# A hand-written order for five engines, listed anew: linear attention and a folded feed-forward on one core

## The chip, the core and the metric

The kernel runs on one core of a Trainium2 chip. A core has five engines with a queue of their own each: TensorE (PE, with its weight loads as PEld), VectorE (DVE), ScalarE (ACT), GpSimd (POOL) and SyncE (SP, which here only issues DMAs). Each engine takes its instructions in the order in which the program lists them, and waits where one needs what another engine has not yet finished. The metric is the device time of one execution in microseconds, as the median of several runs.

## What is computed

```python
q_s = exp(q - max(q, axis=-1)); q_s /= sum(q_s, axis=-1) + 1e-9     # q: 8 x 8 x 576 x 64
k_s = exp(k - max(k, axis=2));  k_s /= sum(k_s, axis=2) + 1e-9
kv  = einsum('bhsd,bhse->bhde', k_s, v)
x   = einsum('bhsd,bhde->bhse', q_s, kv)      # then as 4608 tokens x 512
out = ((x @ w1) * (x @ w2)) @ w3 @ w_out      # w1, w2: 512 x 1024; w3: 1024 x 1024; w_out: 1024 x 512
```

Inputs and output are float32; the kernel works in float16 with float32 sums.

## The kernel before, in words

**The work.** w3 and w_out are folded into one matrix W3O (1024 x 512) first: for each of 8 row blocks ft, PE transposes w3 (step w3t.ft), an engine copies it out of PSUM (w3T.ft), PE multiplies it by w_out in two halves (pf.ft.0, pf.ft.1), and an engine scales it into W3O (W3O.ft).

The attention runs by batch b, 0 to 7. On the side of k: kmx (maximum over the sequence, as a tree of two-input steps for batches 0 to 3, as two reductions kmx.b.0 and kmx.b.1 after that), cba (a transpose and a reduction on DVE), cbx (four small copies on ACT that swap neighbouring groups of 32 partitions, line 509: "ScalarE's swap"), cb (DVE), ksub.b.0 and .1 (subtract), kexp.b.0 and .1 (exponential, ACT), vc.b.0 and .1 (v to float16, from batch 2), kv (PE), kve (ACT) and kv2 (DVE). On the side of q, in two parts p: qmx, qsub, qexp, qsm, qeps, qrc, qn; then q is turned, either on PE with a copy (qt and qT, batches 0 and 1) or by a transposing DMA that SP issues (qd.b.0 and qd.b.1, line 637, from batch 2). Then PE multiplies (xm.b.0, xm.b.1 and xt.b for the last 64 tokens of a batch), and xs and xts copy the result out of PSUM.

The feed-forward runs by chunk c, 0 to 7 for the 512 first tokens of each batch and 8 for the 8 x 64 tokens left. For a chunk there are 8 pairs of steps up.1 and up.0 (x @ w2, x @ w1; 8 matmuls of 256 columns in chunks 0 and 1, 4 of 512 in the others), bs (copies the up.1 product out of PSUM, line 323), ab (multiplies it by the up.0 product, DVE, line 794), and four times down (8 matmuls with W3O, line 801), os (copy out of PSUM) and st (store, two DMAs on SP).

**The order.** Nothing is ordered by the compiler: ORDER (line 77) lists all 794 steps by name, and Plan.run (line 48) emits them in that order, each on its engine. So the list sets the order within each engine's queue and nothing else; between engines only data and buffers order the work. PICKS (line 154) names the engine of those steps that can run on more than one. The buffers are rings: 4 PSUM banks "pab" for up (and for xt from batch 3), 2 "po" for down, pf and xm.b.1, 2 "att" for kv, qt and the other xm, 4 buffers each for bs and os. A step that takes a ring's buffer waits for the reader of its former content.

**The links.** Steps with two inputs in SBUF (kmx as a tree, ksub, qsub, qn, vc on POOL, qeps on DVE) are marked "port". Among the first LINKED steps of the list (line 75), when such a step stands on another engine than the marked step before it, its first instruction is made to wait for the last one of that step (lines 68 to 72, `link` in line 883).

**Loads.** HW lists two loads for SP, LOADS (line 216) those that POOL issues, LATE (line 223) those on SP after that. A load of POOL's list waits for the load eight places ahead of it; the first of LATE waits for the third from the end of LOADS (w1.3 in either order). A load into a buffer in use waits for its readers (line 393). In the names, w3.4 is 512 KB and w3.0 256 KB; loads of q, k and v are 1152 KB per batch.

**Fills.** `fill` (line 347) issues matmuls of zeros that nobody reads; FILL (line 149) puts so many of them ahead of the steps that it names, and "begin" ahead of all.

Of the kernel before, what the change touches and what calls it, by code (L numbers as in the profile page):

```python
# [82 lines left out]
pf.3.0 pf.3.1 kexp.0.1 w3t.1 kexp.0.0 k.2 kv.0 W3O.3 w3T.1 W3O.7 w3T.6 qmx.1.0 kve.0 kv2.0 pf.1.0
pf.6.0 xm.0.0 qsub.1.0 xs.0.0.0 xs.0.0.1 pf.6.1 pf.1.1 kmx.1.0 xm.0.1 qexp.1.0 xs.0.1.1 xs.0.1.0
up.1.0.0.0 bs.0.0.0 up.0.0.0.0 up.1.0.1.0 up.0.0.1.0 up.1.0.0.1 qsm.1.0 qeps.1.0 qrc.1.0 ab.0.0.0
cba.1 w1.3 v.1 q.1.1 qn.1.0 bs.0.1.0 up.0.0.0.1 qt.1.0 ab.0.1.0 up.1.0.1.1 up.0.0.1.1 cbx.1 cb.1
bs.0.0.1 ksub.1.0 ab.0.0.1 qT.1.0 q.2 bs.0.1.1 xt.0 up.1.0.0.2 ab.0.1.1 W3O.6 bs.0.0.2 up.0.0.0.2
ab.0.0.2 W3O.1 ksub.1.1 kexp.1.0 kmx.2.0 up.1.0.1.2 up.0.0.1.2 up.1.0.0.3 bs.0.1.2 up.0.0.0.3
up.1.0.1.3 bs.0.0.3 ab.0.0.3 down.0.0 xts.0.0 kexp.1.1 cba.2 ab.0.1.2 xts.0.1 cbx.2 cb.2 ksub.2.1
kv.1 kve.1 bs.0.1.3 kexp.2.1 os.0.0 down.0.1 ksub.2.0 v.2 up.0.0.1.3 kv2.1 qmx.1.1 xm.1.0 xs.1.0.0  # L90
xs.1.0.1 qsub.1.1 ab.0.1.3 down.0.2 up.1.1.0.0 up.0.1.0.0 up.1.1.0.1 qmx.2.1 qmx.2.0 os.0.1
up.0.1.0.1 bs.1.0.0 up.1.1.0.2 down.0.3 ab.1.0.0 kexp.2.0 qexp.1.1 qsm.1.1 qsub.2.1 k.3 v.3 q.3
qsub.2.0 vc.2.1 vc.2.0 qexp.2.1 qeps.1.1 bs.1.0.1 qexp.2.0 qsm.2.1 qrc.1.1 qsm.2.0 os.0.2 bs.1.0.2
qeps.2.0 up.0.1.0.2 kv.2 kve.2 ab.1.0.1 up.1.1.0.3 up.0.1.0.3 qn.1.1 qrc.2.0 kv2.2 qn.2.0 qeps.2.1
qt.1.16 qt.1.8 os.0.3 ab.1.0.2 bs.1.0.3 qrc.2.1 qn.2.1 st.0.0 k.4 qd.2.0 ab.1.0.3 qT.1.16 down.1.0
qmx.3.1 qT.1.8 qd.2.1 q.4 st.0.1 xm.1.1 down.1.1 xs.1.1.1 xs.1.1.0 xt.1 kmx.3.0 qmx.3.0 up.1.1.1.0
up.0.1.1.0 xts.1.1 xts.1.0 xm.2.0 bs.1.1.0 xs.2.0.0 xs.2.0.1 cba.3 ab.1.1.0 up.1.1.1.1 up.0.1.1.1
bs.1.1.1 ab.1.1.1 os.1.0 cbx.3 st.0.3 v.4 xm.2.1 xs.2.1.1 xs.2.1.0 cb.3 kmx.4.1 up.1.1.1.2
up.0.1.1.2 up.1.1.1.3 bs.1.1.2 vc.3.1 qsub.3.0 qsub.3.1 up.0.1.1.3 ksub.3.0 qexp.3.0 ab.1.1.2
qsm.3.0 bs.1.1.3 qexp.3.1 ab.1.1.3 up.1.2.0.0 up.0.2.0.0 up.1.2.0.1 bs.2.0.0 ksub.3.1 up.0.2.0.1  # L100
vc.3.0 q.5 st.0.2 ab.2.0.0 bs.2.0.1 kexp.3.0 up.1.2.0.2 up.0.2.0.2 up.1.2.0.3 qsm.3.1 ab.2.0.1
qmx.4.1 vc.4.1 up.0.2.0.3 bs.2.0.2 up.1.2.0.4 kexp.3.1 os.1.1 v.5 qeps.3.1 qeps.3.0 kmx.4.0 qsub.4.1
qexp.4.1 kv.3 qrc.3.1 qmx.4.0 ab.2.0.2 down.1.2 down.1.3 os.1.2 qrc.3.0 cba.4 qsm.4.1 bs.2.0.3 kve.3
os.1.3 up.0.2.0.4 up.1.2.0.5 ab.2.0.3 kv2.3 qn.3.1 xt.2 bs.2.0.4 up.0.2.0.5 up.1.2.0.6 qn.3.0
qsub.4.0 cbx.4 cb.4 ab.2.0.4 up.0.2.0.6 qd.3.1 st.1.1 qd.3.0 xts.2.1 qexp.4.0 bs.2.0.5 qmx.5.1
xts.2.0 bs.2.0.6 ab.2.0.5 xm.3.1 xm.3.0 xt.3 ab.2.0.6 xs.3.1.0 xs.3.0.1 xs.3.1.1 xs.3.0.0 xts.3.1
xts.3.0 up.1.2.0.7 up.0.2.0.7 up.1.3.0.0 up.0.3.0.0 bs.2.0.7 qeps.4.1 ksub.4.1 ksub.4.0 vc.4.0
kexp.4.1 qmx.5.0 ab.2.0.7 qrc.4.1 qsm.4.0 qeps.4.0 kexp.4.0 bs.3.0.0 up.1.3.0.1 k.5 kv.4 ab.3.0.0
kmx.5.1 qrc.4.0 q.6 st.1.2 qsub.5.1 st.1.3 st.1.0 up.0.3.0.1 up.1.3.0.2 up.0.3.0.2 down.2.0 down.2.1
k.6 qexp.5.1 bs.3.0.1 kmx.5.0 qmx.6.0 qmx.6.1 cba.5 bs.3.0.2 os.2.0 os.2.1 ab.3.0.2 cbx.5 kve.4 cb.5  # L110
qsub.5.0 ab.3.0.1 kv2.4 up.1.3.0.3 down.2.2 qsm.5.1 qn.4.0 qn.4.1 qd.4.0 qd.4.1 qexp.5.0 st.2.0 q.7
v.6 os.2.2 bs.3.0.3 down.2.3 os.2.3 up.0.3.0.3 qsub.6.0 xm.4.0 ab.3.0.3 xm.4.1 xt.4 xts.4.0 xs.4.1.0
xts.4.1 up.1.3.0.4 up.0.3.0.4 ksub.5.0 vc.5.1 xs.4.0.0 bs.3.0.4 kmx.6.0 ab.3.0.4 qeps.5.1 xs.4.0.1
kexp.5.0 kmx.6.1 xs.4.1.1 up.1.3.0.5 up.0.3.0.5 bs.3.0.5 up.1.3.0.6 up.0.3.0.6 bs.3.0.6 ab.3.0.5
up.1.3.0.7 up.0.3.0.7 qrc.5.1 qsm.5.0 ab.3.0.6 qeps.5.0 bs.3.0.7 qrc.5.0 ksub.5.1 qsub.6.1 kexp.5.1
vc.5.0 up.1.4.0.0 bs.4.0.0 up.0.4.0.0 up.1.4.0.1 st.2.1 qmx.7.1 cba.6 ab.3.0.7 down.3.0 qn.5.1
qsub.7.1 st.2.2 k.7 qmx.7.0 os.3.0 ab.4.0.0 qsub.7.0 qn.5.0 qexp.6.0 qexp.6.1 qsm.6.1 kv.5
up.0.4.0.1 up.1.4.0.2 bs.4.0.2 up.0.4.0.2 down.3.1 cbx.6 bs.4.0.1 ab.4.0.1 os.3.1 qexp.7.0 st.3.1
ab.4.0.2 cb.6 ksub.6.1 qsm.6.0 up.1.4.0.3 bs.4.0.3 up.0.4.0.3 ksub.6.0 qexp.7.1 ab.4.0.3 up.1.4.0.4
kmx.7.1 up.0.4.0.4 kve.5 kexp.6.1 qeps.6.0 bs.4.0.4 qeps.6.1 up.1.4.0.5 kv2.5 up.0.4.0.5 bs.4.0.5  # L120
ab.4.0.4 kexp.6.0 down.3.2 ab.4.0.5 qrc.6.1 qrc.6.0 qsm.7.0 qn.6.1 up.1.4.0.6 os.3.2 kmx.7.0
qeps.7.0 st.2.3 qd.5.0 vc.6.0 qd.5.1 st.3.2 v.7 up.0.4.0.6 bs.4.0.6 xm.5.1 qn.6.0 vc.6.1 xm.5.0
qd.6.1 st.3.0 up.1.4.0.7 xs.5.1.0 xs.5.1.1 ab.4.0.6 up.0.4.0.7 xs.5.0.1 bs.4.0.7 xs.5.0.0 qd.6.0
down.3.3 cba.7 ab.4.0.7 cbx.7 qrc.7.0 qsm.7.1 up.1.5.0.0 os.3.3 st.3.3 up.0.5.0.0 bs.5.0.0 qn.7.0
down.4.0 ab.5.0.0 qeps.7.1 cb.7 down.4.1 os.4.0 ksub.7.1 st.4.0 up.1.5.0.1 ksub.7.0 os.4.1 kexp.7.1
st.4.1 up.0.5.0.1 qrc.7.1 bs.5.0.1 qn.7.1 up.1.5.0.2 kexp.7.0 ab.5.0.1 down.4.2 bs.5.0.2 up.0.5.0.2
os.4.2 st.4.2 kv.6 ab.5.0.2 xt.5 up.1.5.0.3 kve.6 xts.5.0 qd.7.0 xts.5.1 kv2.6 up.0.5.0.3 bs.5.0.3
qd.7.1 vc.7.0 vc.7.1 up.1.5.0.4 ab.5.0.3 up.0.5.0.4 bs.5.0.4 up.1.5.0.5 ab.5.0.4 up.0.5.0.5 bs.5.0.5
up.1.5.0.6 ab.5.0.5 xm.6.0 xm.6.1 bs.5.0.6 xt.6 up.0.5.0.6 xs.6.1.1 xts.6.1 xs.6.1.0 xts.6.0
xs.6.0.0 up.1.5.0.7 xs.6.0.1 ab.5.0.6 up.0.5.0.7 bs.5.0.7 down.4.3 ab.5.0.7 up.1.6.0.0 os.4.3  # L130
down.5.0 st.4.3 bs.6.0.0 up.0.6.0.0 os.5.0 up.1.6.0.1 st.5.0 ab.6.0.0 down.5.1 bs.6.0.1 up.0.6.0.1
os.5.1 st.5.1 up.1.6.0.2 ab.6.0.1 up.0.6.0.2 bs.6.0.2 kv.7 ab.6.0.2 up.1.6.0.3 kve.7 kv2.7 down.5.2
bs.6.0.3 up.0.6.0.3 os.5.2 st.5.2 up.1.6.0.4 ab.6.0.3 up.0.6.0.4 bs.6.0.4 up.1.6.0.5 ab.6.0.4
up.0.6.0.5 bs.6.0.5 up.1.6.0.6 ab.6.0.5 up.0.6.0.6 bs.6.0.6 xm.7.0 xm.7.1 ab.6.0.6 xt.7 up.1.6.0.7
xs.7.1.1 xs.7.0.0 xs.7.1.0 xs.7.0.1 up.0.6.0.7 bs.6.0.7 xts.7.1 xts.7.0 down.5.3 ab.6.0.7 down.6.0
os.5.3 st.5.3 up.1.7.0.0 os.6.0 st.6.0 up.0.7.0.0 bs.7.0.0 up.1.7.0.1 ab.7.0.0 up.0.7.0.1 bs.7.0.1
down.6.1 ab.7.0.1 up.1.7.0.2 os.6.1 st.6.1 down.6.2 bs.7.0.2 up.0.7.0.2 os.6.2 up.1.7.0.3 st.6.2
ab.7.0.2 up.0.7.0.3 bs.7.0.3 up.1.7.0.4 ab.7.0.3 up.0.7.0.4 bs.7.0.4 up.1.7.0.5 ab.7.0.4 up.0.7.0.5
bs.7.0.5 up.1.7.0.6 ab.7.0.5 up.0.7.0.6 bs.7.0.6 up.1.7.0.7 ab.7.0.6 up.0.7.0.7 bs.7.0.7 up.1.8.0.0
# [80 lines left out]
]  # L220
# [699 lines left out]
```

## Time and profile before

| what | before |
|---|---|
| median of 3 runs | 243.56 us (243.51 to 243.75) |
| the profiled execution, its own time | 244.17 us |
| its span in the profile | 242.4 us |
| PE, DVE, ACT, POOL busy | 232.4, 179.7, 123.1, 106.3 us |
| first up step starts | 34.58 us |
| last matmul group starts | 231.25 us, for 7.09 us |
| DMA traffic | 45.67 MB, mean 188 GB/s |

The span runs from the first to the last instruction; what the execution's own time has above it lies around it. Busy times are sums of the instructions' durations. Matmuls overlap in the profile, so that a short gap of PE can hide in its busy time: the distance from one start to the next tells more. A row of the timeline has the start, the duration, the engine, the line, the operation, output and input tiles with shapes, and the number of instructions put together; in square brackets, when the engine was idle before it, for how long and what ended that. A row of a group has the busy time, the mean of one in ns, and the idle time before. "<-DMA qT<-en" means that the transfer which turns q ended the wait.

### The profile page before, as it was taken

To read this page: it belongs to the slowest core of one execution; us is meant where nothing else is said; L and a number is where in the kernel's file an instruction comes from. 1 tells how busy PE (TensorE), PEld (TensorE's weight loads), DVE (VectorE), ACT (ScalarE), POOL (GpSimd) and SP (SyncE) were. 2 spreads that over 40 slices of the span, in tenths; PEclk is the share of its full clock that TensorE was granted. 3 is DMA by queue.
4 is the path that set the end of the run, shared out by engine and by line. 5 is a ranking of instruction groups with operands and counts; after the bars stand their busy time and mean duration, and the time that the engine had idled before them with its cause. 6 is when DMAs were issued, how large, how long until landed. Compare 5 with 4: busy or idle time off the path is not lost.

```text
span 242.4 us, 4971 instructions
## 1 busy us (share of the span) xinstructions
PE 232.4 (96%) x1988; PEld 121.3 (50%) x1988; DVE 179.7 (74%) x270; ACT 123.1 (51%) x228; POOL 106.3 (44%) x72
## 2 busy tenths in 40 slices
...
GB/s 203 218 299 216 334 205 285 268 392 386 367 192 301 302 306 142 353 359 156 360 176 130 176 103 312 107 141 3 95 42 38 60 73 43 0 89 0 63 110 131
DMA packets 37895, 45.67 MB, mean 188 GB/s; under 512 B 15984, under 2 KB 22384, under 8 KB 37872
## 3 DMA queue, kind: packets, MB, share of 16 engines
...
q14 instruction: 8, 0.07, 0.1%
...
## 4 chain that ended last, share of the span: by engine, by line
PE 50%; DVE 18%; DMA 9%; issue 7%; ACT 7%; POOL 6%; DVEq 0%; ACTq 0%; POOLq 0%
PE pab L779 30%; PE po L801 13%; DMA k<-in_k_dram 6%; DVE ab L794 5%; DMA qT<-en 3%; PE po L816 3%; POOL en L614 2%; PE po L452 2%; DVE qr L595 2%; ACT eq L590 2%; DVE qm L577 2%; DVE k L519 2%; ACT mx L509 2%; POOL q L582 1%; ACT bsb L323 1%
## 5 line engine op out<-in xcount | busy, mean ns | idle before, releaser
L794 DVE TENSOR_TENSOR ab<-pab,bsb 128x512 f16<-128x512 f32 x72 | 49.0, 684 | 26.5 <-PE pab L779 25.5
L779 PE MATMUL pab<-x,w2sb 128*128 128x512 f16 (+1 forms) x320 | 66.0, 337 | 0.3 <-DVE bsb L323 0.3
L779 PE MATMUL pab<-x,w1sb 128*128 128x512 f16 (+1 forms) x320 | 65.9, 337 | 0.2 <-DVE ab L794 0.2
L801 PE MATMUL po<-W3O,ab 128*128 128x512 f16 x256 | 59.5, 380 | 0.0
L779 PEld LDWEIGHTS <-w1sb 128*128 128x128 f16 x352 | 34.1, 98 | 27.9 <-issue 0.5
L779 PEld LDWEIGHTS <-w2sb 128*128 128x128 f16 x352 | 33.5, 98 | 28.1 <-issue 1.4
L323 ACT CAST bsb<-pab 128x512 f16<-128x512 f32 x51 | 29.8, 587 | 32.6 <-PE pab L779 32.6
L801 PEld LDWEIGHTS <-ab 128*128 128x128 f16 x256 | 24.6, 98 | 29.1 <-issue 0.4
L323 ACT COPY osb<-po 128x512 f32<-128x512 f32 (+1 forms) x28 | 15.9, 569 | 39.5 <-PE po L801 31.5
L519 POOL TENSOR_TENSOR k<-k,cb 128x1152 f32<-128x1152 f32 x10 | 26.2, 2633 | 13.5 <-DVE k L519 10.4
L614 POOL TENSOR_TENSOR en<-eq,qr 128x1024 f16<-128x1024 f16 (+1 forms) x13 | 27.2, 2106 | 4.4 <-issue 1.2
L582 POOL TENSOR_TENSOR q<-q,qm 128x1280 f32<-128x1280 f32 (+1 forms) x13 | 27.7, 2143 | 2.6 <-issue 1.6
L577 DVE TENSOR_REDUCE qm<-q 128x16 f32<-128x1024 f32 (+1 forms) x16 | 21.2, 1336 | 3.5 <-DMA q<-in_q_dram 3.5
L595 DVE TENSOR_REDUCE qr<-eq 128x16 f32<-128x1024 f16 (+1 forms) x16 | 21.2, 1330 | 2.0 <-ACT eq L590 2.0
L590 ACT ACTIVATE eq<-q 128x1024 f16<-128x1024 f32 (+1 forms) x16 | 18.5, 1164 | 3.7 <-POOL q L582 2.2
L527 ACT ACTIVATE ek<-k 128x1152 f16<-128x1152 f32 x16 | 18.5, 1168 | 3.4 <-DVE k L519 2.8
L323 DVE CAST bsb<-pab 128x512 f16<-128x512 f32 x21 | 14.4, 687 | 3.9 <-PE pab L779 3.3
L484 DVE TENSOR_REDUCE km<-k 128x128 f32<-128x1152 f32 x8 | 17.2, 2154 | 0.0
L452 PE MATMUL po<-wosb,w3T 128*128 128x512 f16 x64 | 15.1, 380 | 0.5 <-ACT w3T L323 0.5
L327 ACT ACTIVATE x<-xm 128x512 f16<-128x512 f32 x16 | 9.1, 602 | 4.8 <-PE xm L662 4.8
L323 DVE COPY osb<-po 128x512 f32<-128x512 f32 x9 | 6.2, 685 | 7.2 <-PE po L801 7.2
L323 POOL CAST v<-v 128x1152 f16<-128x1152 f32 x7 | 9.2, 1314 | 4.1 <-DVE km L496 3.0
...
## 6 DMA issues: line engine op xcount, KB each, us to landing
...
v<-in_v_dram POOLq DMA_DIRECT2D x2, 576.0 KB, 15.2
...
```

The source lines that it names most:

```text
L323: return [(nc.scalar.copy if eng == "ACT" else engine[eng].tensor_copy)(out=out, in_=in_)]
L452: nc.tensor.matmul(st["pf", ft], lhsT=st["w3T", ft][:, gt, :], rhs=wosb[:, gt, :], start=(gt == 0), stop=(gt == N_FT - 1))
L519: return [engine[eng].tensor_tensor(out=kb[:, two(hp), :, :], in0=kb[:, two(hp), :, :], in1=st["cb", b][:, two(hp), None, :].broadcast_to( ...
L527: nc.scalar.activation(out=st["ek", b][:, hp, :, :].rearrange("p j (i d) -> p i j d", i=2), in_=kb[:, two(hp), :, :], func=AF.Exp)
L577: dve.tensor_reduce(out=st["qm", b][:, :, j], in_=qb[:, :, j, :], axis=AX.X, op=ALU.max)
L582: return [engine[eng].tensor_tensor(out=qb[:, :, j, :], in0=qb[:, :, j, :], in1=st["qm", b][:, :, j, None].broadcast_to([P, HH, n, D]), op ...
L590: nc.scalar.activation(out=st["eq", b, p], in_=qb[:, :, j, :], func=AF.Exp)
L595: dve.tensor_reduce(out=st["qr", b][:, :, slice(*PARTS[p])], in_=st["eq", b, p], axis=AX.X, op=ALU.add)
L614: return [engine[eng].tensor_tensor(out=st["en", b][:, j, :, :].rearrange("p j h d -> p h j d"), in0=st["eq", b, p], in1=st["qr", b][:, :, ...
L779: nc.tensor.matmul(st["p", one, c, sub, u][:, a * (t1 - t0):(a + 1) * (t1 - t0)], lhsT=w[:, ct, fb * P:(fb + 1) * P], rhs=x()[:, ct, t0:t1 ...
L794: dve.tensor_tensor(out=st["ab", c][:, nf * u:nf * u + nf, t0:t1], in0=cut(st["p", 0, c, sub, u]), in1=cut(st["bsb", c, sub, u]), op=ALU.mult)
L801: nc.tensor.matmul(st["po", c, tb], lhsT=st["ab", c][:, ft, tb * P:(tb + 1) * P], rhs=W3O[:, ft, :], start=(ft == 0), stop=(ft == N_FT - 1))
```

## The change

The list ORDER is another permutation of the same 794 steps, with PICKS, FILL, LOADS and LATE to match, and LINKED goes from 350 to 580. No step's work is changed. It came from a planning in which ScalarE's swap and the turning transfers had measured lengths; these lengths appear nowhere in the kernel's code.

```diff
-LINKED = 350
+LINKED = 580
...
-q.0.0 q.0.1 w3.0 ident qmx.0.0 qsub.0.0 w3.4 wo.0 wo.1 w3.2 k.0 qmx.0.1 w3.5 w3.3 qexp.0.0 qsm.0.0
+q.0.0 qmx.0.0 qsub.0.0 qexp.0.0 q.0.1 qmx.0.1 qsub.0.1 qexp.0.1 w3.4 w3.0 wo.0 wo.1 w3.2 ident k.0
...
+w3t.5 w3T.5 w3.5 qsm.0.0 w3.3 w3.1 w3t.4 w3t.0 pf.5.0 w3T.0 pf.0.0 qsm.0.1 qeps.0.1 qrc.0.1 qn.0.1
+qeps.0.0 qrc.0.0 v.0 pf.5.1 w3T.4 pf.0.1 w3t.2 w3T.2 W3O.0 W3O.5 qt.0.16 qt.0.8 pf.4.0 qT.0.16
+qT.0.8 pf.4.1 pf.2.0 pf.2.1 q.1.0 k.1 w2.0 qn.0.0 kmx.0.0 cba.0 W3O.2 W3O.4 qt.0.0 w3t.6 w3t.7 w3T.7
...
+bs.0.0.0 up.0.0.1.0 up.1.0.0.1 w1.2 w2.2 k.2 w2.3 kmx.1.0 qsm.1.0 qeps.1.0 qrc.1.0 w1.3 ab.0.0.0
+q.1.1 up.0.0.0.1 bs.0.1.0 qn.1.0 v.1 qt.1.0 W3O.6 cba.1 up.1.0.1.1 bs.0.0.1 cbx.1 ab.0.1.0 cb.1
+ab.0.0.1 bs.0.1.1 ksub.1.1 up.0.0.1.1 qT.1.0 ab.0.1.1 up.1.0.0.2 up.0.0.0.2 xt.0 up.1.0.1.2 bs.0.0.2
+ab.0.0.2 W3O.1 kmx.2.0 q.2 ksub.1.0 bs.0.1.2 up.0.0.1.2 up.1.0.0.3 kexp.1.1 cba.2 up.0.0.0.3
...
+qsm.2.0 k.4 st.0.0 bs.1.0.3 os.0.3 qt.1.16 qT.1.16 ab.1.0.3 qd.2.1 qt.1.8 qeps.2.0 qrc.2.0 down.1.0
+qn.2.0 qT.1.8 xm.1.1 qmx.3.1 qmx.3.0 down.1.1 xs.1.1.0 xs.1.1.1 xt.1 xts.1.1 up.1.1.1.0 qd.2.0
+kmx.3.0 qsub.3.0 qsub.3.1 q.4 st.0.1 v.4 st.0.3 st.0.2 up.0.1.1.0 up.1.1.1.1 up.0.1.1.1 vc.3.1
...
+up.0.2.0.3 up.1.2.0.4 up.0.2.0.4 cbx.4 xts.2.1 qmx.4.1 xts.2.0 xm.3.1 ab.2.0.3 bs.2.0.4 xm.3.0
...
-    "begin": 17, "w3t.4": 8, "qt.0.0": 7,
+    "begin": 17, "pf.5.0": 8,
...
 LOADS = [
-    ("w3", 0), ("w3", 4), ("wo", 0), ("wo", 1), ("w3", 2), ("k", 0), ("w3", 5), ("w3", 3),
+    ("w3", 4), ("w3", 0), ("wo", 0), ("wo", 1), ("w3", 2), ("k", 0), ("w3", 5), ("w3", 3),
     ("w3", 1), ("v", 0), ("q", 1, 0), ("k", 1), ("w2", 0), ("w1", 0), ("w2", 1), ("w1", 1),
-    ("w2", 3), ("w1", 2), ("w2", 2), ("k", 2), ("w1", 3), ("v", 1), ("q", 1, 1),
+    ("w1", 2), ("w2", 2), ("k", 2), ("w2", 3), ("w1", 3), ("q", 1, 1), ("v", 1),
 ]
```

Among the engine choices, by count of steps, before and after: ksub on DVE 6 and 3, on POOL 10 and 13; qn on DVE 3 and 2; vc on POOL 7 and 5, on ACT 5 and 7; xs on DVE 6 and 12, on ACT 26 and 20; bs on DVE 21 and 23; os on DVE 9 and 11. On PE, the steps ahead of xm.3.1 and xm.3.0 lose two pairs of up steps of chunk 2, those ahead of xm.5 four pairs of chunk 4, those ahead of xm.6 five up steps of chunk 5; xm.2.0 has one pair of chunk 1 more ahead of it, kv.1 two steps more. xm.4 and xm.7 have the same steps ahead of them as before, and from xm.7.0 on PE's list is the same. The links among the marked steps are, in the new list: qeps.0.0 to qn.0.0 to kmx.0.0; kmx.1.0 to qn.1.0; ksub.1.1 to kmx.2.0 to ksub.1.0 to ksub.2.0 to ksub.2.1; qn.2.0 to kmx.3.0 to qsub.3.0; and, through the larger LINKED, ksub.6.1 to qeps.6.1 and qn.6.1 to qn.6.0.

133 lines of the change are left out of this document (63 added, 70 removed), and 98 rows, old and new, of the table PICKS.

## The prediction

> **What bounds the kernel now.** First the page's busy times, then the busy times by stretch, then PE's waits.
>
> ```profile
> PE 232.4 (96%) x1988; PEld 121.3 (50%) x1988; DVE 179.7 (74%) x270; ACT 123.1 (51%) x228; POOL 106.3 (44%) x72
> 80.00:90.00 10.00, 10.00 (x117) 4.75 (x115) 10.00 (x13) 8.01 (x12) 8.45 (x5) 1.00 0.88 319
> PE po L662 <- DMA qT<-en: 1.2, 1, 1.2
> PE xm L662 <- DMA qT<-en: 0.6, 1, 0.6
> PE pab L779 <- DVE bsb L323: 0.3, 1, 0.3
> PE pab L779 <- DVE ab L794: 0.2, 1, 0.2
> ```
>
> PE is the bound, and it waits for little: behind the head, 1.2 + 0.6 + 0.3 + 0.2 = 2.3 us in all. Until about 157 us DVE and POOL are full beside it (the second line: DVE 10.00 of 10). So an order can win only those waits and part of the head, and it can lose much, wherever the three full engines get out of step.
>
> Starts in the timeline of PE say more, since a busy PE hides short gaps:
>
> ```profile
> 34.58 1.05 PE L779 MATMUL pab<-x,w2sb 128*128 128x256 f16 x8
> 64.93 1.04 PE L779 MATMUL pab<-x,w1sb 128*128 128x256 f16 x8
> 66.08 0.73 PE L629 MATMUL qtp<-ident,en 128*128 128x128 f16 x10
> 71.71 1.04 PE L779 MATMUL pab<-x,w1sb 128*128 128x256 f16 x8
> 73.37 0.41 PE L662 MATMUL xm<-qT,kv 64*64 64x512 f16 x4 [0.62 <-DMA qT<-en]
> 95.32 1.03 PE L779 MATMUL pab<-x,w1sb 128*128 128x512 f16 x4
> 97.57 0.41 PE L662 MATMUL po<-qT,kv 64*64 64x512 f16 x4 [1.23 <-DMA qT<-en]
> 113.72 1.03 PE L779 MATMUL pab<-x,w1sb 128*128 128x512 f16 x4
> 114.68 0.41 PE L662 MATMUL xm<-qT,kv 64*64 64x512 f16 x4
> 140.42 0.41 PE L662 MATMUL po<-qT,kv 64*64 64x512 f16 x4
> 156.13 1.02 PE L779 MATMUL pab<-x,w2sb 128*128 128x512 f16 x4 [0.35 <-DVE bsb L323]
> 157.33 1.02 PE L779 MATMUL pab<-x,w1sb 128*128 128x512 f16 x4 [0.17 <-DVE ab L794]
> 199.47 10.36 PE pab L779 x48
> ```
>
> The last line (chain of waits) gives the pace: 10.36 / 48 = 0.216 us per matmul, 0.865 per up step. What a start-to-start distance has above 0.865 is lost: 1.15 - 0.87 = 0.28 at 66.08 (turning q of batch 1), 1.66 - 0.87 = 0.79 at 73.37 (xm.2.0), 2.25 - 0.865 = 1.39 at 97.57 (xm.3.1), 0.35 at 156.13 and 1.20 - 0.865 = 0.34 at 157.33. Sum 3.15. The pair at 113.72 has no wait and yet 0.96: 0.1 is the price of the switch to the small form and stays. Three of the five have it: **2.85 us can be had**. From 157 to the end PE runs without a gap, and the change moves only engine choices there.
>
> **The change part by part.** *Fills and transposes ahead.* The seven fills before qt.0.0 go, eight move from w3t.4 to pf.5.0, and the first rows loaded are w3.4. The rows of the head:
>
> ```profile
> 1.55 5.68 PE L350 MATMUL po<-zero 128*128 128x512 f16 x17 [1.55 <-DVE zero L345]
> 7.87 0.71 PE L440 MATMUL w3t<-ident,w 128*128 128x128 f16 x8 [0.63 <-DMA w<-in_moe_w_dram]
> 22.43 1.97 PE L440 MATMUL w3t<-ident,w 128*128 128x128 f16 x24 [0.32 <-DMA w<-in_moe_w_dram]
> 28.98 0.78 PE L544 MATMUL pkv<-v,ek 64*64 64x64 f16 x72
> 4.84 14.64 DMA k<-in_k_dram
> 23.34 0.83 ACT L509 COPY mx<-mx 32x8 f32<-32x8 f32 x4 [0.59 <-DVE mx L503]
> ```
>
> PE waits at 7.87 and at 22.43 for weights; the chain of waits starts from k.0 (4.84 + 14.64 = 19.48). As many bytes go ahead of k.0 as before, so kmx.0.0 starts at 19.5 again. ScalarE's swap (four copies, 0.83) stands in the chain as before; behind it ACT has two evictions fewer ahead of kexp.0.1, so kv.0 comes at 28.8 instead of 28.98 and the first up step at 34.3 instead of 34.58. Bounds: nothing, and 0.3; taken 0.2. New on POOL is qn.0.0 (1.9 us), between w2.0 and w1.0, with links from qeps.0.0 and to kmx.0.0. Behind it in POOL's queue are w1.0 and all later loads. It is hidden: w1.0 needs k.0 landed anyway, at 19.48, and w2.0 was issued about 2 us ahead of that. Without that cover it costs up to its 1.9 us, because kmx.0.0 waits for it.
>
> *Batch 1 on POOL.* ksub.1.0 goes from DVE to POOL and is chained ksub.1.1, kmx.2.0, ksub.1.0, ksub.2.0, ksub.2.1, with alternating engines. Times of the new order that stand without a row, here and below, are laid out by hand from kmx.0.0 at 19.5: each engine's steps in their new order, none before what it needs, each as long as from its start to the next start in the old timeline (on DVE 0.6 for a product or an eviction, 0.08 less than its row has, 2.1 for half a kmx, 2.85 for the tree, 1.1 and 1.4 for the parts of a q reduction; POOL by its rows). With qn.1.0 from 37.1, cb.1 at 41.1 and kmx.2.0 from 44.2 to 47.0, ksub.1.0 ends at 49.6, kexp.1.0 at 50.7. kv.1 is moved behind down.0.1, two more steps, so PE gets there only at 52.4. Behind the waiting ksub.1.0 stand ksub.2.1 and the two qsub on POOL; their reader is kv.2, at 61.0, for which vc.2.0 is ready at 59.6. So the waits cost nothing while 1.4 us of slack lasts.
>
> *Batch 2 and 3.* The durations of POOL and of DVE:
>
> ```profile
> L794 DVE TENSOR_TENSOR ab<-pab,bsb 128x512 f16<-128x512 f32 x72 | 49.0, 684 | 26.5 <-PE pab L779 25.5 <-ACT bsb L323 0.7
> L484 DVE TENSOR_REDUCE km<-k 128x128 f32<-128x1152 f32 x8 | 17.2, 2154 | 0.0
> L519 POOL TENSOR_TENSOR k<-k,cb 128x1152 f32<-128x1152 f32 x10 | 26.2, 2633 | 13.5 <-DVE k L519 10.4 <-DVE cb L515 3.1
> L582 POOL TENSOR_TENSOR q<-q,qm 128x1280 f32<-128x1280 f32 x7 | 16.4, 2343 | 2.4 <-issue 1.6 <-DVE qm L577 0.8
> L614 POOL TENSOR_TENSOR en<-eq,qr 128x1024 f16<-128x1024 f16 x7 | 13.4, 1908 | 2.7 <-ACT bsb L323 1.1 <-ACT mx L509 1.1 <-DVE qr L607 0.4
> 72.77 1.14 POOL L323 CAST v<-v 128x1152 f16<-128x1152 f32 x1 [2.97 <-DVE km L496]
> 90.55 1.91 POOL en L614
> 93.44 1.34 SPq L637 DMA_TRANSPOSE qT<-en x1
> DMA to landing us min/median/max: 3.3/3.5/7.0
> ```
>
> At 72.77 POOL has waited 2.97 for the tree kmx.3.0, by the link; this stays, now with qsub.3.0 behind it. From there to the end of qn.3.0 (90.55 + 1.91 = 92.46, its transfer issued at 93.44) POOL did seven long steps and two vc, and waited some. The new list takes vc.3.1, vc.3.0 and qsub.4.1 from ahead of it (1.14 + 1.14 + 2.34 = 4.6). With kmx.3.0 ending at 71.9 the steps left are 2 x 2.3 + 2 x 1.9 + 2 x 2.6 = 13.6; with 0.6 for cb.3, qn.3.0 ends at 86.1, and with 4.1 to landing (97.57 - 93.44) qT is there at 90.2. PE arrives at 97.57 - 1.39 - 0.79 - 0.28 - 0.3, less four up steps that xm.3.1 is moved ahead of (3.46): 91.4. Margin 1.2: **the 1.39 goes.** xm.2.0 gets two up steps more in front (73.37 - 0.79 - 0.28 - 0.3 + 1.73 = 73.7), while its second transfer, issued when qn.2.0 ends at 68.4, lands at 71.9 with the median 3.5: **the 0.79 goes.** For qt.1.16, qn.1.1 ends at 63.8, PE comes at 65.3: **the 0.28 goes.**
>
> *Batches 4 to 6.* xm.5.1 is moved eight up steps ahead: 140.42 - 2.46 - 0.3 - 6.92 = 130.7. DVE and POOL must be ready that much sooner. Summed over the list ahead of xm.5.1, DVE has 11.0 us less (116.2 for 127.2), POOL 13.6 less (86.1 for 99.7) and ACT 10.7 less: more than the 6.9 that PE has less. Batch 5 itself: kmx.5.1 starts at 101.8, DVE's work from there to qrc.5.0 is 17.8 with about 1.2 of waits, so 120.8; qn.5.0 and qn.5.1 follow (1.9 + 2.3 = 4.2), 125.0; with 3.5 landed at 128.5. Margin 2.2. At xm.6.0 kv2.6 is the last, 154.3 for 155.6. So DVE is no longer behind at 156: **0.35 and 0.34 go.** LINKED = 580 adds but two links here, ksub.6.1 (POOL) to qeps.6.1 (DVE) and qn.6.1 to qn.6.0; DVE comes to the first at 143.8, ksub.6.1 ended at 139, and behind qn.6.0 only batch 7 waits.
>
> *Batch 7.* Both ksub and qn.7.1 go from DVE to POOL (2 x 2.63 + 2.3 = 7.6 us); qT of batch 7 lands at about 181 where PE needs it at 183. In the old order its transfers were issued at 158.03 (below). Hidden by PE's 22 up and 4 down steps between xm.6.0 and xm.7.0; without that cover each us beyond 183 costs one.
>
> **The sum.** 2.85 of waits and 0.2 of the head, less 0.2 for handing over between engines, which I set nowhere else: 2.85. The profiled execution took 244.17 (span 242.4 and 1.8 around it), so it would take 241.3; it stands 0.6 above the median of the runs shown. From the median 243.56: **240.7**. With all bounds on the good side 243.56 - 3.15 - 0.3 = 240.1.
>
> **The rivals.** *A, q turned too late again (chance 0.17).* The margins at xm.3.1 (1.2) and xm.7.0 (2) hold with 3.5 to 4.1 from issue to landing; one transfer took 7.0 (above). At xm.3.1 that is 90.2 + 2.9 = 93.1, a stall of 1.7, and less at the others since PE is then later by itself: 242.4. For it: loads run beside these transfers. Against: three of four pairs land within 3.8.
>
> *B, the array gets slow in the head (0.07).* In the first fence of the head 17 fills take 5.68 us, 0.33 each against 0.216 later: the first half of them ran at half pace. With w3.4, twice the bytes of w3.0, in front, w3t.5 starts one to two us later than 7.87 (an estimate from the bytes), and PE has but transposes from 7.2 (1.55 + 5.68) to about 11. If it falls back, eight fills and some eight fold matmuls cost 0.216 more each, 3.4; the waits for wo.0, at 22.43 and ahead of kv.0 hide 1.5 to 3.4 of it. Price 0 to 1.9, taken 1: 241.7. Against: in the old head the gap of 0.63 did not slow the array.
> The Trainium skill, "TensorE: Matmul & The Clock Gate", Part 1, says that the array falls back to half its clock after an idle window of about 3.4 us, and Part 4 that transposes do not count as busy in the same way. By that rule the stretch from 7.2 to about 11 would be just enough, and the time 241.7; no row of the old trace shows such a stretch.
>
> *C, the change does not do what it says (0.08).* SP's queue is in order. In the old order qn.5.0 was done at 131.0 and its transfer was issued at 135.45:
>
> ```profile
> 129.07 1.91 POOL L614 TENSOR_TENSOR en<-eq,qr 128x1024 f16<-128x1024 f16 x1
> 135.45 2.78 SPq L637 DMA_TRANSPOSE qT<-en x2
> 158.03 2.77 SPq L637 DMA_TRANSPOSE qT<-en x2
> 35.40 0.74 POOL L402 DMA_DIRECT2D v<-in_v_dram x1 [0.96 <-DMA w1sb<-in_moe_w_dram]
> v<-in_v_dram POOLq DMA_DIRECT2D x1, 576.0 KB, 13.3
> DMA to landing us min/median/max: 5.8/9.7/17.1
> ```
>
> If stores or loads hold SP 4.4 us again ahead of a transfer with 1.2 of margin, 3.2 come back and nothing is won: 243.9, within the same. Against: ahead of qd.3 and qd.5 now stand only steps whose readers ended long before.
>
> *D, slower (0.20).* v.1 used to be issued at 35.40, ahead of q.1.1 and qn.1.0. Now it stands behind qn.1.0, which waits for qrc.1.0 and for the tree kmx.1.0 by a new link: 39.0. kv.1 reads it, at 52.4, and all of PE stands behind kv.1. With 13.3 to landing (this transfer, old order) it lands at 52.3; with 17.1 (the longest of v) at 56.1, a stall of 3.7: 240.7 + 3.7 = **244.4**. It decides from 52.4 on, and the kernel is slower once v.1 takes over 16.5. For it: the load comes 3.6 us later, behind a POOL step that waits for DVE. Against: the queue has the same bytes to move in either order, so the last of them should land when the last, q.1.1, did, near 51. Mishaps in other margins of 0.5 (kv.4, the slots of pab near 40) would come on top, and are counted here.
>
> **How the numbers follow.** Forecast 0.48 (240.1 to 241.4), A 0.17, B 0.07, C 0.08, D 0.20. A measurement of this kernel tells about 0.2% (0.5 us) from no change. Faster: 0.48 + 0.17 + 0.07 = 0.72; same: 0.08; slower: 0.20. The range goes from 239.9, a little below the good bounds, to 244.2, inside D: what is left out is most of D.
>
> **What would show it.** Right: PE's waits list qT no more, xm.3.1 starts near 91.5, xm.5.1 near 131, xm.6.0 near 156, and PE's last matmul ends 2.5 to 3 us sooner. Wrong: a wait of PE for v or ek at kv.1 (D), for qT at xm.3.1, xm.5.1 or xm.7.0 (A, C), for DVE's ab or bsb between 40 and 115 (my sums of DVE are too short), or more than 0.35 us per fill in the second batch of fills (B).

## The result, and the profile after

The new order takes **240.96 us** (median of 4 runs, 240.52 to 241.12) against 243.66 for the old one (243.51 to 244.01, 4 runs): a ratio of 0.9885, 95% interval 0.9867 to 0.9902, 2.7 us less. The forecast was 240.7. The profiled execution of the new order took 240.52 with a span of 238.4; it is the lowest of its four, so its distance from the old profile's span (4.0) overstates the gain.

First the busy times of the new kernel and the chain that ended last, from its page:

```profile
PE 230.7 (97%) x1981; PEld 121.1 (51%) x1981; DVE 180.0 (76%) x275; ACT 120.7 (51%) x221; POOL 112.8 (47%) x74
...
PE 86%; DMA 5%; DVE 3%; POOL 2%; issue 1%; ACT 1%; POOLq 0%; ACTq 0%
```

DVE's and ACT's sums are what they were, within 2.4; POOL has 6.5 more (it has three ksub and one qn more than before, and two vc fewer). The work has not shrunk, and the chain that ended last is now 86% PE. The old page's row for that chain:

```profile
PE 50%; DVE 18%; DMA 9%; issue 7%; ACT 7%; POOL 6%; DVEq 0%; ACTq 0%; POOLq 0%
```

What DVE, POOL and ACT had in it is nearly gone: they deliver in time. PE's waits, the new kernel's (line, total, times, longest):

```profile
PE po L350 <- DVE zero L345: 1.6, 1, 1.6
PE w3t L440 <- DMA w<-in_moe_w_dram: 1.4, 2, 1.0
PE pkv L544 <- ACT ek L527: 0.7, 1, 0.7
PE po L452 <- DMA wosb<-in_moe_w_out_dram: 0.5, 1, 0.5
```

All four are in the head. The 1.2 and 0.6 for qT, the 0.3 for bsb and the 0.2 for ab are gone. The starts in PE's timeline, in the new order:

```profile
34.36 1.05 PE L779 MATMUL pab<-x,w2sb 128*128 128x256 f16 x8
...
65.59 0.72 PE L629 MATMUL qtp<-ident,en 128*128 128x128 f16 x10
67.97 0.41 PE L662 MATMUL xm<-qT,kv 64*64 64x256 f16 x8
...
72.96 1.04 PE L779 MATMUL pab<-x,w1sb 128*128 128x256 f16 x8
73.93 0.41 PE L662 MATMUL xm<-qT,kv 64*64 64x512 f16 x4
...
91.65 0.41 PE L662 MATMUL po<-qT,kv 64*64 64x512 f16 x4
...
131.01 0.41 PE L662 MATMUL po<-qT,kv 64*64 64x512 f16 x4
...
154.99 0.41 PE L662 MATMUL xm<-qT,kv 64*64 64x512 f16 x4
...
227.95 7.09 PE L816 MATMUL po<-W3O,ab 128*128 128x512 f16 x40
```

and three starts of the old order that belong beside them (xm.1.1, xm.6.0 and the last group):

```profile
68.46 0.41 PE L662 MATMUL xm<-qT,kv 64*64 64x256 f16 x8
...
162.60 0.41 PE L662 MATMUL xm<-qT,kv 64*64 64x512 f16 x4
...
231.25 7.09 PE L816 MATMUL po<-W3O,ab 128*128 128x512 f16 x40
```

xm.2.0 starts 0.97 behind the up step before it, where it was 1.66. Correcting each old start for the up steps that xm is moved ahead of or behind (0.865 each, 0.875 in chunk 1), PE is ahead of its old self by 0.22 at the first up step, 0.49 at xm.1.1, 1.19 at xm.2.0, 2.46 at xm.3.1, 2.49 at xm.5.1 and 3.29 at xm.6.0, and stays there: 3.30 at the last group. So between the first up step and the last group the time came from the places named before, and from no other: batch 1 0.27, xm.2.0 0.70, xm.3.1 1.27, around 156 us 0.80.

What feeds xm.3.1 and xm.5.1, in POOL's and SP's timeline of the new kernel:

```profile
82.20 4.20 POOL L614 TENSOR_TENSOR en<-eq,qr 128x1280 f16<-128x1280 f16 x2
...
84.56 3.11 SPq L637 DMA_TRANSPOSE qT<-en  x2
...
121.04 4.20 POOL L614 TENSOR_TENSOR en<-eq,qr 128x1024 f16<-128x1024 f16 x2 [4.04 <-DVE qr L607]
```

POOL ends qn.3.0 at 86.4, where it ended at 92.46; the second transfer of batch 3 lands at 89.5, 2.1 ahead of PE.

### The profile page after: what moved, and what is told of

Same layout as the page of the kernel before. It is cut to its first block, busy times and chain, and to the rows that moved or that the text cites. A ratio compares the mean times of both kernels' runs of the same rounds, so it can differ in the third digit from the quotient of the medians.

```text
span 238.4 us, 4957 instructions
## 1 busy us (share of the span) xinstructions
PE 230.7 (97%) x1981; PEld 121.1 (51%) x1981; DVE 180.0 (76%) x275; ACT 120.7 (51%) x221; POOL 112.8 (47%) x74
## 4 chain that ended last, share of the span: by engine, by line
PE 86%; DMA 5%; DVE 3%; POOL 2%; issue 1%; ACT 1%; POOLq 0%; ACTq 0%
PE pab L779 52%; PE po L801 23%; DMA wosb<-in_moe_w_out_dram 5%; PE po L816 3%; PE pkv L544 2%; PE po L452 2%; PE xm L662 1%; DVE k L519 1%; POOL en L614 1%; POOL w L402 1%; PE po L662 1%; DVE kmx L493 1%; ACT ek L527 0%; PE pkv L554 0%; PE qtp L629 0%
## 5 line engine op out<-in xcount | busy, mean ns | idle before, releaser
L323 ACT CAST bsb<-pab 128x512 f16<-128x512 f32 x49 | 28.3, 585 | 36.5 <-PE pab L779 36.2
L519 POOL TENSOR_TENSOR k<-k,cb 128x1152 f32<-128x1152 f32 x13 | 33.9, 2626 | 8.1 <-DVE km L496 3.5
L614 POOL TENSOR_TENSOR en<-eq,qr 128x1024 f16<-128x1024 f16 (+1 forms) x14 | 29.2, 2093 | 17.4 <-DVE qr L607 8.0
L323 ACT COPY osb<-po 128x512 f32<-128x512 f32 (+1 forms) x26 | 14.9, 576 | 35.8 <-PE po L801 28.9
L323 DVE COPY osb<-po 128x512 f32<-128x512 f32 (+1 forms) x11 | 7.3, 667 | 20.8 <-PE po L801 13.7
L323 DVE CAST bsb<-pab 128x512 f16<-128x512 f32 x23 | 15.8, 687 | 2.7 <-PE pab L779 2.2
L327 ACT ACTIVATE x<-xm 128x512 f16<-128x512 f32 x14 | 7.9, 596 | 5.5 <-PE xm L662 5.4
L350 PE MATMUL po<-zero 128*128 128x512 f16 x25 | 8.4, 509 | 1.6 <-DVE zero L345 1.6
```

The source lines that it names most:

```text
L323: return [(nc.scalar.copy if eng == "ACT" else engine[eng].tensor_copy)(out=out, in_=in_)]
L519: return [engine[eng].tensor_tensor(out=kb[:, two(hp), :, :], in0=kb[:, two(hp), :, :], in1=st["cb", b][:, two(hp), None, :].broadcast_to( ...
L614: return [engine[eng].tensor_tensor(out=st["en", b][:, j, :, :].rearrange("p j h d -> p h j d"), in0=st["eq", b, p], in1=st["qr", b][:, :, ...
```

## The experiments

To compare kernels with different heads, the span is cut in three: up to the first up step, from there to the start of the last group of matmuls (L816; called the **body** here), and the rest. Both marks are starts in PE's timeline, as quoted for the two kernels. The body turns out to be repeatable to 0.02 us: it is 193.58 to 193.60 in five kernels that leave the new list alone where it matters (e1, e5, e6, e8, e12) as well as in the new kernel itself, 193.59.

Each ratio compares a kernel with executions of the old one taken beside it, whose medians were 243.66 (beside the new kernel), 244.03 (e1 to e4), 243.88 (e5 to e8) and 243.87 (e9 to e12). Below, "slower" and "less than the old kernel" are meant against these.

| kernel | median, us (range, runs) | ratio to old, 95% interval | first up | last group | body |
|---|---|---|---|---|---|
| old | 243.66 (243.51 to 244.01, 4) | 1 | 34.58 | 231.25 | 196.67 |
| new | 240.96 (240.52 to 241.12, 4) | 0.9885 [0.9867, 0.9902] | 34.36 | 227.95 | 193.59 |
| e1 new, LINKED 350 | 241.11 (240.87 to 241.24, 4) | 0.9881 [0.9864, 0.9897] | 34.93 | 228.53 | 193.60 |
| e2 old, LINKED 580 | 244.09 (243.78 to 244.78, 12) | 1.0008 [0.9993, 1.0022] | 34.17 | 231.10 | 196.93 |
| e3 new, POOL's old work | 243.02 (242.64 to 244.65, 8) | 0.9968 [0.9948, 0.9988] | 34.74 | 230.40 | 195.66 |
| e4 old, POOL's new work | 248.75 (247.53 to 250.09, 6) | 1.0188 [1.0150, 1.0227] | 34.34 | 237.49 | 203.15 |
| e5 new, no fills ahead of pf.5.0 | 240.69 (240.25 to 240.81, 4) | 0.9871 [0.9857, 0.9884] | 34.14 | 227.72 | 193.58 |
| e6 new, v.1 later | 240.96 (240.89 to 241.05, 4) | 0.9885 [0.9872, 0.9899] | 34.77 | 228.36 | 193.59 |
| e7 old, batch 7 to POOL | 243.24 (242.86 to 243.46, 9) | 0.9969 [0.9954, 0.9984] | 34.38 | 230.16 | 195.78 |
| e8 new, head rearranged | 241.37 (240.66 to 241.58, 4) | 0.9895 [0.9877, 0.9914] | 35.17 | 228.76 | 193.59 |
| e9 old, batch 3's q first | 244.15 (243.76 to 244.41, 12) | 1.0003 [0.9982, 1.0023] | 34.24 | 231.96 | 197.72 |
| e10 new, kmx.4 first on DVE | 242.94 (242.77 to 244.90, 12) | 0.9971 [0.9940, 1.0002] | 34.88 | 230.35 | 195.47 |
| e11 old, three edits | 244.34 (244.26 to 244.56, 12) | 1.0016 [0.9999, 1.0032] | 34.40 | 232.35 | 197.95 |
| e12 new, vc.3 on POOL | 240.77 (240.45 to 240.86, 6) | 0.9865 [0.9842, 0.9888] | 34.94 | 228.53 | 193.59 |

**The links, e1 and e2.**

```diff
-LINKED = 580
+LINKED = 350
```

> The new list with the old LINKED of 350, so that the links added behind batch 3 (qn.2.0 to kmx.3.0 to qsub.3.0, ksub.6.1 to qeps.6.1, qn.6.1 to qn.6.0, and those near batch 2) go as far as the 350 first steps do not hold them. Theory (the gain comes from the list: q is turned in time because POOL does less ahead of qn): 240.7 to 241.3, within 0.3 of the new kernel, PE's waits unchanged. Rival (the links themselves bring the gain, by keeping DVE and POOL from slowing each other): 1 to 3 us slower than the new kernel, 242 to 244, and DVE's two-input steps of the batches 2 to 6 get longer beside POOL's.

and the reverse in the old kernel:

> The old list with LINKED 580; five links more, among them vc.4.0 (POOL) to qeps.4.0 (DVE) to qsub.5.1 and qn.6.1 to qeps.7.0 to vc.6.0. Theory (links bring next to nothing by themselves): within 0.3 of the old kernel, 243.4 to 244.0; PE's wait for qT at xm.3.1 (1.2 in the old profile) stays as it is. Rival (links bring the gain): 242.5 or less. Second rival (a link makes POOL wait for a busy DVE): 244.3 or more.

Without the added links the new body is 193.60, the same; with them the old one is 196.93, 0.26 longer, and its waits for qT are still there (1.5 and 1.0 in total). So the larger LINKED brings nothing. This says less than the expectation of e1 claims: qn.2.0, kmx.3.0 and qsub.3.0 stand at places 231, 243 and 244 of the new list, so they stay linked at 350. By the lists and the engine choices, e1 takes away just two links, ksub.6.1 to qeps.6.1 and qn.6.1 to qn.6.0, and e2 adds five. The nine links among the first 350 steps of the new list stand in every version of it here, and what they bring or cost is open.

**POOL's work ahead of qn.3, e3 and e12.** e3 puts vc.3 back on POOL and two steps back ahead of qn.3.1:

```diff
-"vc_3_1": "ACT"
-"vc_3_0": "ACT"
+"vc_3_1": "POOL"
+"vc_3_0": "POOL"
...
-bs.2.0.2 qn.3.1 kmx.4.1
+bs.2.0.2 qmx.4.1 qsub.4.1 qn.3.1 kmx.4.1
```

(qmx.4.1 and qsub.4.1 are gone from their later places.)

> The new kernel, but POOL gets its old work back ahead of qn.3: vc.3.1 and vc.3.0 on POOL, and qmx.4.1 with qsub.4.1 ahead of qn.3.1. Nothing else moves. Theory: POOL has 1.14 + 1.14 + 2.34 = 4.6 more ahead of qn.3.0, which ends at 91.0 instead of 86.4; its transfer lands 3.1 to 4.1 later, at 94.1 to 95.1, while PE wants it at 91.65: a wait of 2.5 to 3.4 for qT at xm.3.1 and 243.4 to 244.4, as slow as the old kernel. Rival (the gain lies elsewhere, in the head or in DVE's lighter load): within 0.8 of the new kernel, at most 241.8.

e12 does the first half alone:

> The new kernel with vc.3.1 and vc.3.0 on POOL again, and nothing else: half of the POOL work that was put back before. The new profile has qT of batch 3 landed near 89.5 and read at 91.65, a margin of 2.1. Theory of the margin: 2 x 1.14 = 2.3 more on POOL ahead of qn.3.0 eats the margin and no more, a wait of 0 to 0.4, so 240.7 to 241.4. Rival (each microsecond of POOL costs PE in proportion, 2.06 for 4.6): 1.0 more than the new kernel, 242.0.

PE's and POOL's timeline of e3:

```profile
84.34 2.35 POOL L582 TENSOR_TENSOR q<-q,qm 128x1280 f32<-128x1280 f32 x1
86.64 4.21 POOL L614 TENSOR_TENSOR en<-eq,qr 128x1280 f16<-128x1280 f16 x2
93.99 0.41 PE L662 MATMUL po<-qT,kv 64*64 64x512 f16 x4 [1.89 <-DMA qT<-en]
```

and of e12, SP and PE:

```profile
86.93 3.10 SPq L637 DMA_TRANSPOSE qT<-en  x2
92.23 0.41 PE L662 MATMUL po<-qT,kv 64*64 64x512 f16 x4
```

In e3 qn.3.0 ends at 90.85 (91.0 expected) and the wait for qT is back. It is 1.89 and not 2.5 or more, because the head of this execution was 0.4 later, and PE with it, and the transfer landed at 93.99, 0.1 ahead of the times expected. The body grows by 2.07, two thirds of the whole gain. In e12, with half of that work, the second transfer lands 0.3 ahead of PE, and the body is the new one's to the hundredth. So it is a margin: 2.3 us of POOL cost nothing, 4.6 cost 2.07. The theory held in e12. In e3 its mechanism held, but the wait (1.89) and the time (243.02) came out under their ranges.

**POOL alone in the old order, e4.**

```diff
-"vc_3_1": "POOL"
-"vc_3_0": "POOL"
+"vc_3_1": "ACT"
+"vc_3_0": "ACT"
...
-kmx.4.0 qsub.4.1 qexp.4.1 kv.3 qrc.3.1
+kmx.4.0 qrc.3.1
...
-up.1.2.0.6 qn.3.0 qsub.4.0
+up.1.2.0.6 qn.3.0 qsub.4.1 qexp.4.1 qsm.4.1 qsub.4.0
```

(kv.3 stands behind down.1.3, and qsm.4.1 is gone from its old place.)

> The old kernel with only POOL's part of the change ahead of qn.3: vc.3.1 and vc.3.0 on ScalarE, qsub.4.1 (with its qexp.4.1 and qsm.4.1) behind qn.3.0, kv.3 two down steps later. Theory: the gap of 1.39 at xm.3.1 goes and nothing takes its place: 242.1 to 242.7, 1.0 to 1.5 less than the old kernel. Rival (DVE is the bound behind it, until 157 us, and PE only waits later): 243.3 to 243.8, with the waits for ab and bsb near 156 longer by what was won.

It became 4.7 us slower, and 3.5 to 3.6 in the two executions that list the full clock (247.5 and 247.7); both expectations failed. The rows of e4, from the timelines of DVE, POOL, ACT and PE:

```profile
86.46 2.15 DVE L484 TENSOR_REDUCE km<-k 128x128 f32<-128x1152 f32 x1
88.53 0.26 DVE L607 RECIPROCAL qr<-qr 128x20 f32<-128x20 f32 x1
...
88.94 4.21 POOL L614 TENSOR_TENSOR en<-eq,qr 128x1280 f16<-128x1280 f16 x2 [5.79 <-DVE qr L607]
...
95.47 1.27 ACT L590 ACTIVATE eq<-q 128x1280 f16<-128x1280 f32 x1 [2.24 <-POOL q L582]
...
99.49 1.87 PE L779 MATMUL pab<-x,w1sb 128*128 128x512 f16 x4 [3.84 <-ACT bsb L323]
```

POOL was free 5.79 us earlier and could do nothing with it, because on DVE qrc.3.1 stands behind kmx.4.0. So qsub.4.1 came late, ACT waited for it at qexp.4.1, and behind qexp.4.1 in ACT's queue stood the bs that PE needed. The wait for qT had turned into one three times as long.

**DVE's order, e10.** In the new kernel, DVE's order alone is put back:

```diff
-ab.2.0.0 qrc.3.0 up.1.2.0.1
+ab.2.0.0 up.1.2.0.1
...
-bs.2.0.1 qrc.3.1 bs.2.0.2 qn.3.1 kmx.4.1 kmx.4.0 qn.3.0
+bs.2.0.1 bs.2.0.2 kmx.4.1 kmx.4.0 qrc.3.0 qrc.3.1 qn.3.1 qn.3.0
```

> The new kernel with one thing put back as in the old list, on DVE: the two reductions kmx.4.1 and kmx.4.0 ahead of qrc.3.0 and qrc.3.1 instead of behind them. POOL's and ScalarE's lists are the new ones. Theory (DVE's order is as needed as POOL's): qrc.3.1 comes 4.2 later, at 85.9, and with it qn.3.0's end, at 90.4; qT lands 3.1 later, 93.5, while PE wants it at 91.65: a wait of 1.9, 242.4 to 243.0. Rival (only POOL's amount of work counts): within 0.4 of the new kernel.

PE's timeline of e10 has the wait that was expected:

```profile
94.05 0.41 PE L662 MATMUL po<-qT,kv 64*64 64x512 f16 x4 [1.81 <-DMA qT<-en]
```

The body grows by 1.88, and the wait is 1.81 (1.9 expected). Two different edits on two engines each bring back the same wait: in the new list q of batch 3 is in time only if both engines come to its steps early enough.

**The two gaps near 156, e7.**

```diff
-"ksub_7_1": "DVE", "ksub_7_0": "DVE", "qn_7_1": "DVE"
+"ksub_7_1": "POOL", "ksub_7_0": "POOL", "qn_7_1": "POOL"
```

> The old kernel with ksub.7.1, ksub.7.0 and qn.7.1 on POOL instead of DVE, nothing else. Theory (the two gaps of 0.35 and 0.34 near 156 are there because DVE is behind): DVE has some 5 us less ahead of 156, the gaps go, 0.6 to 0.8 less than the old kernel: 242.9 to 243.1. Rival (it is not DVE's load but the order of bs and ab at that place, or POOL's own steps hold DVE's): within 0.3 of the old kernel.

Busy times from 140 to 157 us (PE, PEld, DVE, ACT, POOL, then granted clock, DMA share, GB/s), of the old kernel:

```profile
140.00:157.00 17.00, 16.65 (x159) 7.58 (x157) 16.86 (x24) 9.77 (x19) 9.09 (x5) 1.00 0.70 183
```

and of e7, with the starts of xm.5.1 and xm.6.0 in e7:

```profile
140.00:157.00 17.00, 17.00 (x161) 7.87 (x161) 13.36 (x27) 9.65 (x18) 14.75 (x8) 1.00 0.75 194
```

```profile
140.11 0.41 PE L662 MATMUL po<-qT,kv 64*64 64x512 f16 x4
...
161.51 0.41 PE L662 MATMUL xm<-qT,kv 64*64 64x512 f16 x4
```

DVE goes from full to 13.36 of 17, POOL had room for the work (9.09 of 17 before), and PE has no wait there. From xm.5.1 to xm.6.0 PE takes 21.40 (140.11 to 161.51) where it took 22.18 (140.42 to 162.60): 0.78, as the new order wins at this place (0.80). This term needs nothing but three engine choices. The theory held: 0.64 less than the old kernel, of 0.6 to 0.8 expected (the time itself, 243.24, lies above 242.9 to 243.1, as the old kernel beside it took 243.88).

**The forecast's other ways, e5 and e6.** e5 takes away the eight fills, e6 issues v.1 later:

```diff
-    "begin": 17, "pf.5.0": 8,
+    "begin": 17,
```

> The new kernel without the eight fills ahead of pf.5.0 (they are zeros that nobody reads). The new kernel's profile has these fills at 1.89 for 8, 0.236 each, so the array was not slow there. Forecast's theory (the array stays at its pace without them, and the waits for weights at 15.2 and 23.4 hide what they took): 240.6 to 241.2, no difference over 0.3. Rival (they keep the array awake through the transposes): the fold's matmuls near 11 to 20 take 0.4 each instead of 0.2, and the time is 0.3 to 1.9 longer, 241.3 to 242.9.

```diff
-bs.0.1.0 qn.1.0 v.1 qt.1.0
+bs.0.1.0 qn.1.0 qt.1.0
...
-ksub.1.1 up.0.0.1.1
+ksub.1.1 v.1 up.0.0.1.1
```

> The new kernel with v.1 issued five steps later on POOL's list, behind ksub.1.1 instead of behind qn.1.0: at about 43.8 instead of 38.95. In the new profile it took 12.1 to landing. If that time is the transfer's own (rival D of the forecast, the mechanism by which the change could have been slower): it lands at 55.9, kv.1 wants it at 52.6, a wait of 3.3 and 244.2. If the time is the queue's, with all bytes ahead of it to move in either case: it lands near 51 to 52 and the time is within 0.3 of the new kernel. Halfway between (576 KB at the rate of the queue when it has nothing else): 6 to 9 to landing, 50 to 53, at most 0.4 slower.

PE's timeline of e5, and then the transfers issued from 34 to 56 us in the new kernel and from 44 to 60 in e6 (KB, us from issue to landing):

```profile
8.81 2.02 PE L440 MATMUL w3t<-ident,w 128*128 128x128 f16 x24 [1.61 <-DMA w<-in_moe_w_dram]
12.56 1.89 PE L452 MATMUL po<-wosb,w3T 128*128 128x512 f16 x8 [1.73 <-DMA wosb<-in_moe_w_out_dram]
```

```profile
v<-in_v_dram POOLq DMA_DIRECT2D x1, 576.0 KB, 12.1
```

```profile
v<-in_v_dram POOLq DMA_DIRECT2D x1, 576.0 KB, 6.8
```

e5: the eight fold matmuls after the transposes take 1.89, 0.236 each, with or without the fills ahead of them, and the time is not told apart from the new kernel's. In this execution 5.4 us with nothing but transposes on PE (7.2 to 12.56) did not slow the array, where rival B's working had 3.8 us as just enough. e6: v.1 was issued at 38.95 and landed at 51.05; issued at 44.41 it lands at 51.2. So the 12.1 is not the transfer's own length; that the rest of it is the wait for bytes queued ahead agrees with both rows. The mechanism of rival D falls.

**The head, e8.**

```diff
-pf.7.0 w3t.1
+pf.7.0 pf.7.1 w3t.1
...
-ksub.0.1 kexp.0.1 ksub.0.0 kexp.0.0 qT.0.0 w3T.6 W3O.3 w3T.1 W3O.7 kv.0
+ksub.0.1 w3T.6 kexp.0.1 ksub.0.0 W3O.7 kexp.0.0 qT.0.0 W3O.3 w3T.1 pf.6.0 kv.0
```

> The new kernel with four steps moved in the head, so that PE has work while it waits 0.69 for kexp.0 at kv.0: pf.7.1 right behind pf.7.0, w3T.6 and W3O.7 between ACT's and DVE's other steps sooner, pf.6.0 ahead of kv.0. Theory (the head's last wait can be filled): the wait at 28.77 goes, the first up step starts 0.2 to 0.6 sooner, 240.4 to 240.8 for 241.0. Rival (the weights are the limit: w1.3 landed at about 46.3 and is needed at 46.5): the wait only moves to the first up step that reads w1.3, and the time is within 0.2 of the new kernel. It is also the candidate for a version faster than both.

Theory and rival both fell: the first up step starts at 35.17, later than in any other kernel, and no wait came up behind it (the body is 193.59). The edit was built on the 0.69 at kv.0 in the new kernel's profile; in five other kernels whose head is the new one's (e1, e3, e6, e10, e12) that wait is 0.29 to 0.30. What differs is the wait for w3 near 23 us: 0.40 in the new kernel's profile, 0.86 to 1.08 in those five and 0.95 here. PE's timeline of e1 has it:

```profile
22.86 1.70 PE L440 MATMUL w3t<-ident,w 128*128 128x128 f16 x24 [1.08 <-DMA w<-in_moe_w_dram]
```

Against those five, e8 is still 0.2 to 0.4 later. It has one pf step less behind kv.0, and xm.0.0 starts 1.18 behind the start of the four matmuls ahead of it, which need 0.87. No version tried beats the new kernel by more than the intervals leave open.

**The old order mended by hand, e9 and e11.** e9 puts the steps of batch 3's q first on all three engines:

```diff
-ab.2.0.1 qmx.4.1 vc.4.1
+ab.2.0.1 qeps.3.1 qeps.3.0 qrc.3.1 qrc.3.0 qmx.4.1 vc.4.1
...
-kmx.4.0 qsub.4.1 qexp.4.1 kv.3
+kmx.4.0 kv.3
...
-qn.3.0 qsub.4.0 cbx.4 cb.4 ab.2.0.4 up.0.2.0.6
+qn.3.0 qsub.4.1 qexp.4.1 qsub.4.0 cbx.4 cb.4 ab.2.0.4 qsm.4.1 up.0.2.0.6
```

> The old list with the steps of batch 3's q put first on all three engines: qeps.3 ahead of vc.4.1 on ScalarE, qrc.3 ahead of qmx.4.1 and kmx.4.0 on DVE, qsub.4.1 behind qn.3.0 on POOL, and its readers qexp.4.1 and qsm.4.1 correspondingly later. vc.3 stays on POOL. Theory, as mended by the run that moved POOL's steps alone (the path to q's turn runs over ScalarE, DVE and POOL, and all three queues have to be rearranged): qn.3.0 ends near 88.6, qT lands near 92 to 93, PE comes at 96.2, the 1.39 goes: 242.3 to 243.0, that is 0.9 to 1.6 under the old kernel. Rival (DVE's load bounds the old order from 70 to 157 anyway, so that a gap closed at 97 opens again later): within 0.4 of the old kernel, with longer waits for ab and bsb near 156.

e11 adds xm.2.0 two up steps later and e7's choices:

> The old list with three edits: batch 3's q first on ScalarE, DVE and POOL (1.39 at xm.3.1), xm.2.0 with its xs two up steps later (0.79 at xm.2.0), ksub.7 and qn.7.1 on POOL (0.69 near 156). The 786 or so other steps keep their old places, LINKED is 350, the head and the loads are the old ones. Theory (the gain is these gaps and nothing else): 0.3 of the 2.87 is the price of the switch to the small form, so 2.3 to 2.7 under the old kernel, 241.1 to 241.6. Rival (the new list as a whole lightens DVE, and single gaps come back elsewhere): 242.3 or more, with new waits for ab, bsb or qT.

Both gave nothing: ratios of 1.0003 and 1.0016. PE no longer waits for qT of batch 3. What it waits for is in the timelines of ACT, DVE and PE of e9:

```profile
92.20 1.28 ACT L590 ACTIVATE eq<-q 128x1280 f16<-128x1280 f32 x1
93.50 0.82 ACT L509 COPY mx<-mx 32x8 f32<-32x8 f32 x4
...
94.35 0.17 DVE L513 TENSOR_REDUCE mxe<-mx 128x8 f32<-128x16 f32 x1 [2.36 <-ACT mx L509]
...
95.50 1.46 DVE L595 TENSOR_REDUCE qr<-eq 128x20 f32<-128x1280 f16 x1
96.88 1.47 DVE L577 TENSOR_REDUCE qm<-q 128x20 f32<-128x1280 f32 x1
98.27 1.27 DVE L794 TENSOR_TENSOR ab<-pab,bsb 128x512 f16<-128x512 f32 x2
...
95.63 1.02 PE L779 MATMUL pab<-x,w1sb 128*128 128x512 f16 x4 [0.68 <-DVE ab L794]
96.58 0.41 PE L662 MATMUL po<-qT,kv 64*64 64x512 f16 x4
...
99.00 1.02 PE L779 MATMUL pab<-x,w2sb 128*128 128x512 f16 x4 [1.74 <-DVE ab L794]
```

qexp.4.1, pushed back, stands ahead of ScalarE's swap; DVE idles 2.36 for the swap's result, and the two q reductions that then follow stand ahead of two ab. PE waits 0.68 and 1.74 for those: 2.42 in place of 1.39, and the body is 1.05 longer. e11 repeats these two waits (0.67 and 1.74), wins its 0.78 near 156 (21.40 from xm.5.1 to xm.6.0), and at batch 2 gets 0.68 of wait for an xs in place of the 0.62 for qT. So e9's rival is right in effect: the gap opens again, though at once and not near 156. That the old order could not be mended by some other few edits is not shown.

## Why the prediction was right, and where it was not

- **The bound and the gaps (2.85): right.** The body is 3.08 shorter. The four places gave 0.27, 0.70, 1.27 and 0.80, against 0.18, 0.69, 1.29 and 0.69 by the forecast's terms. The first and the last are mis-sized, by 0.1 each; e7 wins 0.78 at the last place. e3 and e10 show the cause at xm.3.1, e7 the one at 156. For batch 1 and xm.2.0 the new trace agrees, and no experiment took them apart, so 0.97 of the 3.08 rests on that trace alone.
- **The times worked out by hand: right to 0.7 us, except one.** Forecast and trace: qn.3.0's end 86.1 and 86.4, qT landed 90.2 and 89.5, xm.3.1 91.4 and 91.65, xm.2.0 73.7 and 73.93, qn.5.1's end 125.0 and 125.2, xm.5.1 130.7 and 131.0, xm.6.0 155.6 and 155.0, v.1's issue 39.0 and 38.95. The exception is v.1's landing, 52.3 and 51.05, on the safe side.
- **A reading that does not hold:** DVE and POOL are not both full until 157. In the old kernel's stretches of 10 us from 50 to 130, DVE is busy 8.15 to 10.00 and POOL 7.23 to 10.00; from 150 to 160 POOL has 1.36. The term near 156 could be won because POOL had room.
- **Handing over between engines (less 0.2): wrong, it is 0.** The body holds just the closed gaps.
- **The head (0.2 sooner): wrong in sign.** In the new kernel's profile it came out (34.36 for 34.58), but this execution was a lucky one. Over the six profiles with the old list's head the first up step starts at 34.35 in the mean (34.17 to 34.58), over the six with the new one's (new, e1, e3, e6, e10, e12) at 34.77 (34.36 to 34.94): 0.4 later. The step that failed is the chain to kv.0: the forecast let it start from k.0 alone and put the loads of w3 at nothing. In the traces of e1, e6, e10 and e12 that chain starts from a load of w3 issued at 5.61: w3t starts at 22.73 to 22.87 (22.07 to 22.50 in the six of the old list), and w3T.7 stands ahead of cb.0 in DVE's queue and waits for it, 1.01 to 1.12. So cb.0's first instruction comes at 24.63 to 24.80 (old list 23.78 to 24.20) and kv.0 at 29.17 to 29.35 (28.57 to 28.98). Why these loads land later in the new order is open.
- **How it fits.** 3.08 less the 0.4 of the head is 2.7, the measured difference, but two more terms hide in it. What an execution's own time has above its span, which the forecast carried over as 1.8, is 1.72 to 1.84 in every execution of the old list and its variants, and 2.06 to 2.16 in those of the new one (1.86 to 1.95 in e3 and e12, which have vc.3 on POOL): 0.3 lost outside the span. And the stretch behind the last group is 10.4 to 10.5 in all eight profiles of the new list, but 11.0 to 11.15 in three of the old list's six (old, e2, e7) and 10.4 to 10.5 in the other three: 0.3 won in the mean. The cause of either is open. So the body came out 0.4 better than the 2.65 forecast (2.85 less 0.2) and the head 0.6 worse, and the two other terms, which the forecast did not have, cancel: that 240.7 came so near to 240.96 is in part luck.
- **Rival A** (a turn that comes too late) did not happen. The margin at xm.3.1 was 2.1 (forecast 1.2), at xm.7.0 1.9 (forecast 2), and e3 shows what it costs when it is used up.
- **Rival B** did not happen: the eight fills took 1.89 in the new kernel, whose four executions list a mean granted clock of 0.999 to 1.0. **Rival C** neither: qT of batch 3 was issued at 84.56, with the end of qn.3.1. **Rival D**, to which 0.20 was given, was reasoned against rightly (the queue has the same bytes to move in either order): e6 shows it. By its own numbers (52.4 + 2.85 - 39.0) the kernel would have been slower from 16.3 us to landing on, not 16.5; it took 12.1.
- The forecast's premise for LINKED, that the two links added by the larger number hold nothing up, is shown by e1.
